# A fused attention and gated feed-forward kernel on one core: which part of w_down the second token block takes first, and where its combinations are formed

## The chip, the core and the metric

The kernel runs on one core of one Trainium2 chip. Five engines work side by side: TensorE (PE) does the matrix products, VectorE (DVE), ScalarE (ACT) and GpSimd (POOL) do the elementwise work, SyncE (SP) issues the DMAs. Matrix products land in PSUM; the other data lies in SBUF. The metric is the device time of one launch in microseconds (us), the median over several runs. The time before is 2574.85 us (three runs, 2573.92 to 2575.61).

## What is computed

All in float32, with S = 2048 tokens, D = 576, 32 heads of 18 and F = 4608:

```python
xn = layernorm(A_x)
s  = attention(xn, A_wqkv) @ A_wo              # 32 heads, softmax over all 2048 keys
g  = silu((gelu(xn @ B_w_gate) * (xn @ B_w_up)) @ B_w_down)
out = A_x + s * g
```

## The kernel before

**Tiling.** A prologue normalises x and projects q, k and v. After it, everything goes by sections. The 2048 tokens are cut into 4 blocks b of 512. The 4608 hidden columns are cut into 18 parts r of 256, each of two groups g of 128. One section is the gate and the up product of one group for one block: 27 pairs of matmuls (line 412, outputs pg and pu). There are 4 x 18 x 2 = 144 sections, in the order block, place within the block, group. Sections 11 to 138 also carry attention. Between their pairs stand eight score products (pe, line 861), whose exponential ScalarE takes (pT, line 862), and eight products for the row maxima of a later group of heads (pm, line 809), which VectorE reduces (mx, line 811). After the pairs come 32 matmuls of probabilities by values (acc, line 878). PE is programmed by hand, in the order written; in this middle stretch SP is too. The order on ACT, DVE and POOL is made there by a planner, which keeps a written order only for the instructions that are marked for it. In the epilogue all engines run in the written order.

**The ring.** pe, pm, acc and the outputs py of the down product share three PSUM buffers (`ring`, line 394). A matmul waits until an older tile has been read out of its buffer. pg and pu have two other buffers each.

**The down product.** The product with w_down is done for one part at a time, after the pairs and the acc matmuls of the section that follows the part's second group (`downs`, line 625). It goes by a scheme of seven products for a 2 x 2 split of tokens and columns (`PRODUCTS`, line 53). Seven sums of the two groups' activations (`sums_a`, `cut_a`, on POOL) meet seven combinations of the w_down quarters, held as high and low parts in the one tile T. Each of the seven py tiles is added by VectorE into one of seven accumulators M (line 527); at the first place of a later block ScalarE copies it into M instead (line 525), which starts the accumulators anew. Before that copy the accumulators of the block just finished must be combined by eight additions (`COMBINED`, line 58, done by `combine`, line 542) into four quarters of the block's result, and the quarters 6, 4, 1 and 5 must be stored to the DRAM tensor ys (line 553).

**Where T comes from.** In block 0 the first five parts (`PLAIN` = 5) are multiplied without the scheme. For the parts in `FORMED` the combinations are formed on the core. The raw w_down part is loaded (`load_rawd`), POOL makes the sums (`sums_b`, lines 475 to 477), ACT writes the high parts (`high_b`, lines 483 to 486), POOL the low parts (`low_b`, lines 491 to 494), and four DMAs store T to the DRAM tensor ts (`t_piece`, line 468). `FORMED` holds places 5 to 17 of block 0 and places 0 to 4 of block 1. Everywhere else T is loaded from ts by four DMAs.

**The turn of a block.** Place 17 of a block is multiplied after the first section of the next one. The eight additions on M are then hung into the following section and the stores behind it; the section after that ends with the copies into M. At the turns from block 1 to 2 and from 2 to 3 all eight additions go to POOL (lines 532 to 535) and all four stores are issued together. At the turn from block 0 to 1 POOL gets four of them and VectorE the other four: one at pair 14 of the same section (line 537), three at pairs 2, 8 and 13 of the section after (lines 560 and 561). The stores of quarters 1 and 5 come between the two sections, those of 6 and 4 at pair 19 of the second (line 562).

**Spare work.** From attention section `SCALED` on, every second section takes one job into two borrowed tiles: scaling an attention result, or the gate (silu) of one group of 128 rows of ys. What isn't done in this way is left to the epilogue, where `gate(k)` (line 1021) does it for row group k unless it is among the first `gated`.

**The epilogue.** It does the last sections, the last three down products and sixteen output steps. `step()` (line 1053) projects 128 rows with w_o (po, 28 matmuls, line 1036), lets VectorE multiply by the gate and add x (lines 1045 to 1050), and prepares the operand for two steps later (`split_o`: oh on ACT, ol on DVE). Lines 1161 to 1174 are the end: the last down product with eight additions on M, step 9, one gate, step 10, then the four quarters of the last block with the steps 11 to 15 between them.

Of the kernel before, what the change touches and what calls it, by code (L numbers as in the profile page):

```python
# [17 lines left out]
P = 128  # L18
NT = S // P
TB = 512  # L20
# [17 lines left out]
G = 2  # L38
NR = F // (G * P)
NF = NB * NR * G  # L40
FIRST = (0, 0, 3, 5, 3, 5, 3, 6, 4, 6, 5)
# [4 lines left out]
DC, TH = D // 2, TB // 2  # L46
ENDS = NF - len(FIRST) - NU * NA
PLAIN = len(FIRST) // G
FORMED = [(0, r) for r in range(PLAIN, NR)] + [(1, r) for r in range(PLAIN)]
NEXT = [(0, r) for r in range(1, PLAIN)] + FORMED + [(0, NR)]  # L50
OTS = (4, 9, 0, 5)
SCALED = G * (NR + PLAIN) - len(FIRST) + 1
PRODUCTS = ((2, (0, 6)), (5, (1, 3)), (3, (2, 5)), (6, (3, 4)), (0, (4, 2)), (4, (5, 1)), (1, (6, 0)))
SHARED = 8
QUARTERS = ((0, 0, 6), (0, 1, 4), (1, 0, 1), (1, 1, 5))
# [4 lines left out]
GC = 0.044715  # L60
GS = 0.7978845608028654
SCALE = DH ** -0.5


def f(ap):
# [16 lines left out]
def kernel(ctx: ExitStack, tc: tile.TileContext, x, wqkv, wo, w_gate, w_up, w_down, out):  # L82
    nc = tc.nc
# [42 lines left out]
    def load_gu(t, keep=lambda i: i):  # L126

        raw = raw_tile([P, NC, P])
        for a, w in enumerate((w_gate, w_up)):
            keep(nc.sync.dma_start(raw[HR * a:HR * a + HR], w[:, t * P:(t + 1) * P].rearrange("(k p) n -> p k n", p=HR)))  # L130
        return raw, [], []
# [382 lines left out]
    def down(b, r, then={}):  # L514
        if b == 0 and r < PLAIN:
            return down_plain()
        (ah, al), T, M = FF["A"], FF["T"], FF["M"]
        for m, (i, k) in PRODUCTS:
            py = ring("py")
            for t in range(2):  # L520
                tt = slice(t * P, (t + 1) * P)
                for n, (h, w) in enumerate(((ah, 0), (ah, 1), (al, 0))):
                    nc.tensor.matmul(py[:, t, 0:DC], h[:, i, tt], T[:, w, k], start=n == 0, stop=n == 2)  # L523
            if r == 0:
                nc.scalar.activation(M[:, m], py[:, :, 0:DC], AF.Copy)
            else:
                nc.vector.tensor_tensor(M[:, m], py[:, :, 0:DC], M[:, m], op=ALU.add)  # L527
            for eng, to, op, by in then.get(m, ()):
                eng.tensor_tensor(M[:, to], M[:, to], M[:, by], op=op)  # L529
        if r == NR - 1 and b < NB - 1:  # L530
            FF["gates"].append(b)
            for k, (p, q) in enumerate(COMBINED):
                combine_at(6 * k + 6, nc.gpsimd, q)
                if b > 0:
                    combine_at(6 * k + 6, nc.gpsimd, p)
            if b == 0:
                combine_at(14, nc.vector, COMBINED[0][0])

    def combine_at(i, eng, what):
        FF["hooks"].setdefault(i, []).append(lambda: combine(eng, *what))  # L540
# [3 lines left out]
        M = FF["M"]  # L544
        tc.keep_in_program_order(eng.tensor_tensor(M[:, to], M[:, to], M[:, by], op=op))

    def store_gates(b, some=range(7)):

        for i, c, m in QUARTERS:
            if m not in some:  # L550
                continue
            rows = slice(b * TB + TH * i, b * TB + TH * i + TH)
            nc.sync.dma_start(ys[rows, DC * c:DC * c + DC].rearrange("(t p) d -> p t d", p=P), FF["M"][:, m])

    def gates():

        for b in FF["gates"]:
            if b == 0:
                store_gates(b, (1, 5))
                for i, k in ((2, 1), (8, 2), (13, 3)):  # L560
                    combine_at(i, nc.vector, COMBINED[k][0])
                FF["hooks"].setdefault(19, []).append(lambda b=b: store_gates(b, (4, 6)))
            else:
                store_gates(b)
        FF["gates"] = []

    def load_rawd(r):
        FF["rawd"] = ffn.tile([P, G, D], F32, name="rawd")
        nc.sync.dma_start(FF["rawd"], w_down[r * G * P:(r + 1) * G * P, :].rearrange("(g p) n -> p g n", p=P))

    def section(specials=(), tag="f", slots=False, tail=0):

        n = FF["n"]
        FF["n"] += 1
        b, r = divmod(n // G, NR)
        g = n % G
        keep = tc.keep_in_program_order
        pairs, pg, pu = gate_up(tag)
        hooks, FF["hooks"] = FF["hooks"], {}

        def hook(i, what):
            hooks.setdefault(i, []).append(what)

        for i in range(n + 1, min(n + 3, NF)):
            if i not in FF["raw"]:
                FF["raw"][i] = load_gu(i % (NR * G))
        nxt = FF["raw"].pop(n + 1, None)
        one = split_ap if n + 1 < ATT.start else split
        if nxt:
            for k in range(NG - 1):  # L590
                split_gu(nxt, k, one)
        if n == 0:
            load_rawd(0)
        if g == 0 and (b, r) in FORMED:
            raw = FF["rawd"]
            hook(22 if r == 0 else 12, lambda: sums_b(raw))
        new = n + 1 < NF and (n + 1) % (NR * G) == 0
        xd = []
        if new:
            for k in range(NG - 1):  # L600
                hook(9 * k + 9, lambda k=k: xd.append(load_xd(b + 1, k)))
        for p in spread(pairs, specials, 1 if slots else None, hooks, tail):
            p()
        if nxt:
            split_gu(nxt, NG - 1, one)
        FF["w"] = nxt
        if new:
            copy_xd(xd[0], 0, keep)
        FF["act"] = activate(pg, pu, g, n < ATT.stop)
        for t in FF.pop("late", ()):  # L610
            t()
        if g > 0 or n not in ATT:
            FF.pop("last", lambda: None)()
        if new:
            xd.append(load_xd(b + 1, NG - 1, 2))
            for t in hooks.get(len(pairs), ()):
                t()
            for i in range(XG):
                FF["hooks"].setdefault(2 + 2 * i, []).append(lambda i=i: copy_xd(xd[1], 0, keep, i))
            for k in range(NG - 1):  # L620
                for i in range(XG):
                    copy_xd(xd[k], 1, keep, i)
            FF["xd"] = xd
# [5 lines left out]
    def finish():  # L629

        n = FF["n"] - 1
        b, r = divmod(n // G, NR)
        g, h = n % G, FF["act"]
        pool, vec, act = nc.gpsimd, nc.vector, nc.scalar
        keep = tc.keep_in_program_order
        FF.pop("last", lambda: None)()

        def hook(i, what):
            FF["hooks"].setdefault(i, []).append(what)

        def behind(what):
            what(keep if (n + 1) % (NR * G) == 0 else lambda i: i)

        if g == 1 and (b, r + 1) in NEXT:
            load_rawd((r + 1) % NR)
        if b == 0 and r < PLAIN:
            if g == 0:
                raw = FF["rawd"]
                hook(4, lambda: cut_plain_b(raw))
            cut_plain(g, h)  # L650
        elif (b, r) in FORMED:
            lead = n < ATT.start
            if g == 0:
                high_b(0)
                high_b(1)
                hook(2, lambda: low_b(0))
                hook(10, lambda: low_b(1))
                for k, i in enumerate((13, 20)):
                    hook(i, lambda k=k: t_piece(r, k, True))
                sums_a(g, h, vec if lead else pool)  # L660
                hook(12, lambda: cut_a(0, h, pool, pool, keep))
            else:
                for k, i in enumerate((2, 9)):
                    hook(i, lambda k=k: t_piece(r, 2 + k, True))
                behind(lambda k: (sums_a(g, h, pool, k), cut_a(1, h, pool, pool, keep)))
        else:
            if g == 0:
                late = (n + 2) % (NR * G) == 0 and n + 2 < NF
                for k, i in enumerate((None, 5, 27, 27) if late else (None, 5, 13, 21)):
                    if i is None:  # L670
                        t_piece(r, k)
                    else:
                        hook(i, lambda k=k: t_piece(r, k))
            behind(lambda k: (sums_a(g, h, pool, k), cut_a(g, h, pool, pool, k)))
        if g == G - 1:
            FF["down"].append((b, r, n + 1))
# [298 lines left out]
    with tc.tile_pool(name="epi", bufs=1, reuse_waits="tile") as epi:  # L975
# [87 lines left out]
            n += 1  # L1063

        def load_raw(n):
            FF["raw"][n] = load_gu(n % (NR * G))

        def last_section(tag):

# [87 lines left out]
        for k in range(3):  # L1157
            step()
            if k == 0:
                cut_a(1, h, act, pool)  # L1160
        last_down(2, {0: ((pool, 5, ADD, 0), (pool, 5, ADD, 2)),
                      1: ((vec, 6, SUB, 3), (vec, 6, ADD, 0), (pool, 5, SUB, 1), (vec, 6, SUB, 4), (vec, 4, ADD, 2), (pool, 1, SUB, 3))})
        step()
        gate(gated)
        step()
        M = FF["M"]
        for i, c, m in QUARTERS:
            t = ffn.tile([P, 2, DC], F32, name="tg", tag=("h0", "h1")[c], bufs=2 - c)
            act.activation(t, M[:, m], AF.Tanh, scale=0.25)
# [33 lines left out]
```

## Time and profile before

| what | value |
|---|---|
| median of three runs | 2574.85 us |
| the profiled execution's own time | 2575.34 us |
| its span, first to last instruction | 2573.6 us |
| PE busy | 2546.1 us, 99% |
| VectorE busy | 2089.8 us, 81% |
| GpSimd busy | 1640.2 us, 64% |
| ScalarE busy | 1464.9 us, 57% |

Times within the trace count from the first instruction. Matmuls are pipelined, so the end of one overlaps the start of the next, and a row's duration is that of one instruction and not its share of the engine. In a row of a timeline the bracket says how long the engine sat idle before the instruction and what released it. In a row of the windows view a stretch is followed by its length, then by busy time and count of instructions on PE, PE's weight loads, DVE, ACT and POOL, then by the granted TensorE clock as a share of full speed, the share of DMA time and GB/s. In the list of waits the numbers are us in total, times, and the longest.

### The profile page before, as it was taken

How to read it: one execution, taken by the hardware profiler on the slowest of the kernel's cores; microseconds unless marked ns; L12 is line 12 of the kernel's file. 1: busy time of each engine (PE TensorE's matmuls, PEld its weight loads, DVE VectorE, ACT ScalarE, POOL GpSimd, SP SyncE). 2: the span in 40 equal slices, each digit the busy share in tenths (PEclk: the TensorE clock that was granted, in tenths of full speed). 3: DMA queues.
4: the chain of work that ended last, by engine and by line, in shares of the span. 5: the costliest groups of instructions: out<-in, count | busy, mean ns of one | idle time of the engine just before them, and what ended most of it. 6: DMA issues, size and time to landing. Idle time of an engine off the chain costs nothing. (4 is left out here: it accounts for less than half of the span.)

```text
span 2573.6 us, 52904 instructions
## 1 busy us (share of the span) xinstructions
PE 2546.1 (99%) x20548; PEld 1838.3 (71%) x20548; DVE 2089.8 (81%) x2360; ACT 1464.9 (57%) x1772; POOL 1640.2 (64%) x1710
## 2 busy tenths in 40 slices
PE   9999999999999999999999999999999999999998
PEld 8888766676666666667766677666666776666788
DVE  5325888898887888888887898888888888888367
ACT  3224366666666656666566566555566665555621
POOL 3105588888888866666567565666667665656773
PEclk9999999999999999999999999999999999999999
DMA  8855455555575546767777666666668767665675
GB/s 263 270 184 134 103 163 160 166 166 169 159 202 171 169 136 162 170 167 167 171 185 199 168 168 169 165 169 158 162 156 210 170 169 170 170 160 152 187 210 209
DMA packets 410465, 447.47 MB, mean 174 GB/s; under 512 B 107108, under 2 KB 286820, under 8 KB 410216
## 3 DMA queue, kind: packets, MB, share of 16 engines
q1 hardware_dynamic: 410216, 444.09, 65.1%
q8 instruction: 164, 2.69, 0.5%
q14 instruction: 85, 0.70, 0.1%
HBM read 347.59 MB, written 96.38 MB: 173 GB/s over the span
## 5 line engine op out<-in xcount | busy, mean ns | idle before, releaser
L862 ACT ACTIVATE pT<-pe 128x1024 f32<-128x1024 f32 x1024 | 1047.4, 1026 | 582.6 <-PE pe L861 548.7
L811 DVE TENSOR_REDUCE mx<-pm 128x2 f32<-128x1024 f32 x1024 | 1221.4, 1224 | 179.8 <-PE pm L809 163.6
L412 PE MATMUL pu<-xd,wh 64*128 64x512 f32 x2538 | 926.5, 396 | 1.6 <-DVE t L426 1.6
L412 PE MATMUL pg<-xd,wh 64*128 64x512 f32 x2538 | 926.2, 396 | 1.9 <-ACT t L425 1.9
L412 PEld LDWEIGHTS pg<-xd,wh 64*128 64x128 f32 x2538 | 468.0, 184 | 114.3 <-issue 56.9
L412 PE MATMUL pg<-xd,wl 64*128 64x512 f32 x1269 | 496.6, 391 | 1.1 <-POOL wl L117 1.1
L412 PE MATMUL pu<-xd,wl 64*128 64x512 f32 x1269 | 496.2, 391 | 0.0
L412 PEld LDWEIGHTS pu<-xd,wh 64*128 64x128 f32 x2538 | 468.0, 184 | 29.6 <-DVE t L426 2.9
L878 PE MATMUL acc<-pT,VS 128*32 128x512 f32 x4096 | 466.0, 595 | 0.0
L110 POOL TENSOR_SCALAR wh<-raw 128x384 fp32r<-128x384 f32 x402 | 216.3, 540 | 386.1 <-PE pu L412 264.3
L112 POOL TENSOR_TENSOR wl<-raw,wh 128x384 fp32r<-128x384 f32 x402 | 414.3, 1033 | 27.8
L809 PE MATMUL pm<-KA,QT 64*128 64x512 f32 x2048 | 414.4, 394 | 6.9 <-ACT pT L862 5.0
L861 PE MATMUL pe<-QT,KA 64*128 64x512 f32 x2048 | 411.3, 393 | 4.0 <-DVE mx L811 3.7
L523 PE MATMUL py<-T,ah 128*128 128x288 f32 x1876 | 381.6, 299 | 2.2 <-DVE yy L1045 1.4
L527 DVE TENSOR_TENSOR M<-py,M 128x576 f32<-128x576 f32 x448 | 338.8, 757 | 31.9 <-PE py L523 18.2
L523 PEld LDWEIGHTS py<-T,ah 128*128 128x128 f32 x1876 | 298.8, 188 | 57.1 <-issue 55.6
L441 POOL TENSOR_TENSOR al<-h,ah 128x512 fp32r<-128x512 f32 (+1 forms) x143 | 295.6, 2067 | 64.0 <-ACT ah L438 52.4
L878 PEld LDWEIGHTS acc<-pT,VS 128*32 128x32 f32 x4096 | 120.0, 109 | 276.8 <-issue 229.8
L861 PEld LDWEIGHTS pe<-QT,KA 64*128 64x128 f32 x2048 | 193.4, 184 | 115.8 <-DVE mx L811 32.1
L523 PE MATMUL py<-T,al 128*128 128x288 f32 x938 | 276.1, 294 | 0.0
L412 PEld LDWEIGHTS pg<-xd,wl 64*128 64x128 f32 x1269 | 234.3, 185 | 31.8 <-POOL wl L117 2.0
L412 PEld LDWEIGHTS pu<-xd,wl 64*128 64x128 f32 x1269 | 234.3, 185 | 15.0
(169 smaller groups left out, 2917.5 us busy)
## 6 DMA issues: line engine op xcount, KB each, us to landing
T<-ts SPq DMA_DIRECT2D x98, 576.0 KB
KA<-qk SPq DMA_DIRECT2D x768, 72.0 KB
T<-ts SPq DMA_DIRECT2D x98, 432.0 KB
raw<-in_B_w_gate_dram SPq DMA_DIRECT2D x144, 288.0 KB
raw<-in_B_w_up_dram SPq DMA_DIRECT2D x144, 288.0 KB
ts<-T SPq DMA_DIRECT2D x36, 576.0 KB
VS<-vs SPq DMA_DIRECT2D x128, 152.0 KB
qk<-t SPq DMA_DIRECT2D x72, 256.0 KB
```

The lines of the kernel that those rows point to most:

```text
L110: first = nc.gpsimd.tensor_scalar(hi, raw, 1.0, 1.0, op0=ALU.mult, op1=ALU.mult)
L112: keep(nc.gpsimd.tensor_tensor(lo, raw, f(hi), op=ALU.subtract))
L412: nc.tensor.matmul(o, w[1 + wp][k][rr, c, :], xd[k][xp][rr, c, :], start=(i == 0), stop=(i == len(terms) - 1))
L441: keep(two.tensor_tensor(lo, raw, f(hi), op=ALU.subtract))
L523: nc.tensor.matmul(py[:, t, 0:DC], h[:, i, tt], T[:, w, k], start=n == 0, stop=n == 2)
L527: nc.vector.tensor_tensor(M[:, m], py[:, :, 0:DC], M[:, m], op=ALU.add)
L809: nc.tensor.matmul(pm[:, a], QS[u, r][rr, t * P:(t + 1) * P], KS[(u * NA + c) % KB][r][rr, :], start=True, stop=True)
L811: return nc.vector.tensor_reduce(MX[u][:, 2 * r:2 * r + 2, t, c], pm, axis=AX.X, op=ALU.max)
L861: nc.tensor.matmul(pe[:, a], KS[(u * NA + c) % KB][r][rr, t * P:(t + 1) * P], QS[u, r][rr, :], start=True, stop=True)
L862: nc.scalar.activation(PT[u, kt][:, 2 * r:2 * r + 2, :], pe, AF.Exp, scale=SCALE)
L878: nc.tensor.matmul(ACC[u][32 * a:32 * a + 32, :], VS[(u * NA + c) % VB][:, v:v + 32], pt[:, a, :], start=first, stop=last, skip_group_chec ...
```

## The change

The first place of block 1 takes part 5, whose combinations were stored in block 0; places 1 to 5 take parts 0 to 4. So place 0 of block 1 loads T, and places 1 to 5 form it. The turn from block 0 to 1 is written like the other two: eight additions on POOL, four stores together. The spare jobs start two sections later. At the end the additions on M are spread behind the steps 9 and 10, and a gate stands behind each of these two steps.

```diff
-FORMED = [(0, r) for r in range(PLAIN, NR)] + [(1, r) for r in range(PLAIN)]
-NEXT = [(0, r) for r in range(1, PLAIN)] + FORMED + [(0, NR)]
+FORMED = [(0, r) for r in range(PLAIN, NR)] + [(1, r) for r in range(1, PLAIN + 1)]
+NEXT = [(0, r) for r in range(1, PLAIN)] + FORMED
-SCALED = G * (NR + PLAIN) - len(FIRST) + 1
+SCALED = G * (NR + PLAIN + 1) - len(FIRST) + 1
+def part(b, r):
+    return r if b != 1 or r > PLAIN else r - 1 if r > 0 else PLAIN
+
+def gu_part(n):
+    return G * part(*divmod(n // G, NR)) + n % G
...
                 combine_at(6 * k + 6, nc.gpsimd, q)
-                if b > 0:
-                    combine_at(6 * k + 6, nc.gpsimd, p)
-            if b == 0:
-                combine_at(14, nc.vector, COMBINED[0][0])
+                combine_at(6 * k + 6, nc.gpsimd, p)
...
         for b in FF["gates"]:
-            if b == 0:
-                store_gates(b, (1, 5))
-                for i, k in ((2, 1), (8, 2), (13, 3)):
-                    combine_at(i, nc.vector, COMBINED[k][0])
-                FF["hooks"].setdefault(19, []).append(lambda b=b: store_gates(b, (4, 6)))
-            else:
-                store_gates(b)
+            for i, c, m in QUARTERS:
+                rows = slice(b * TB + TH * i, b * TB + TH * i + TH)
+                nc.sync.dma_start(ys[rows, DC * c:DC * c + DC].rearrange("(t p) d -> p t d", p=P), FF["M"][:, m])
...
-            hook(22 if r == 0 else 12, lambda: sums_b(raw))
+            hook(12, lambda: sums_b(raw))
...
-        g, h = n % G, FF["act"]
+        g, h, s = n % G, FF["act"], part(b, r)
...
-            load_rawd((r + 1) % NR)
+            load_rawd(part(b, r + 1))
...
-                    hook(i, lambda k=k: t_piece(r, k, True))
+                    hook(i, lambda k=k: t_piece(s, k, True))
...
-        last_down(2, {0: ((pool, 5, ADD, 0), (pool, 5, ADD, 2)),
-                      1: ((vec, 6, SUB, 3), (vec, 6, ADD, 0), (pool, 5, SUB, 1), (vec, 6, SUB, 4), (vec, 4, ADD, 2), (pool, 1, SUB, 3))})
+        last_down(2, {0: ((pool, 5, ADD, 0), (pool, 5, ADD, 2)), 1: ((vec, 6, SUB, 3), (pool, 5, SUB, 1), (vec, 6, ADD, 0))})
+        M = FF["M"]
+
+        def add(eng, to, op, by):
+            eng.tensor_tensor(M[:, to], M[:, to], M[:, by], op=op)
+
         step()
-        gate(gated)
+        add(pool, 1, SUB, 3)
+        add(vec, 6, SUB, 4)
+        gate(n)
         step()
-        M = FF["M"]
+        add(vec, 4, ADD, 2)
+        gate(n)
```

Elsewhere `load_gu(i % (NR * G))` becomes `load_gu(gu_part(i))`, and the loads from ts take `part(b, r)` in place of `r`.

More of the change, by code (lines that the diff above doesn't have):

```diff
@@ L545, in combine @@
         tc.keep_in_program_order(eng.tensor_tensor(M[:, to], M[:, to], M[:, by], op=op))
[L547 to L553, printed above, removed]
     def gates():
         for b in FF["gates"]:
-            if b == 0:
-                store_gates(b, (1, 5))
-                for i, k in ((2, 1), (8, 2), (13, 3)):
-                    combine_at(i, nc.vector, COMBINED[k][0])
-                FF["hooks"].setdefault(19, []).append(lambda b=b: store_gates(b, (4, 6)))
-            else:
-                store_gates(b)
+            for i, c, m in QUARTERS:
+                rows = slice(b * TB + TH * i, b * TB + TH * i + TH)
+                nc.sync.dma_start(ys[rows, DC * c:DC * c + DC].rearrange("(t p) d -> p t d", p=P), FF["M"][:, m])
         FF["gates"] = []
@@ L585, in section @@
             if i not in FF["raw"]:
-                FF["raw"][i] = load_gu(i % (NR * G))
+                FF["raw"][i] = load_gu(gu_part(i))
         nxt = FF["raw"].pop(n + 1, None)
@@ L663, in finish @@
                 for k, i in enumerate((2, 9)):
-                    hook(i, lambda k=k: t_piece(r, 2 + k, True))
+                    hook(i, lambda k=k: t_piece(s, 2 + k, True))
                 behind(lambda k: (sums_a(g, h, pool, k), cut_a(1, h, pool, pool, keep)))
@@ L670, in finish @@
                     if i is None:
-                        t_piece(r, k)
+                        t_piece(s, k)
                     else:
-                        hook(i, lambda k=k: t_piece(r, k))
+                        hook(i, lambda k=k: t_piece(s, k))
             behind(lambda k: (sums_a(g, h, pool, k), cut_a(g, h, pool, pool, k)))
@@ L1065, in load_raw @@
         def load_raw(n):
-            FF["raw"][n] = load_gu(n % (NR * G))
+            FF["raw"][n] = load_gu(gu_part(n))
         def last_section(tag):
```

## The prediction

> **What bounds the kernel now.** I read the busy shares first, then PE's waits around the turns of the blocks, and then measured each section from the first acc matmul of one section to that of the next.
>
> ```profile
> PE 2546.1 (99%) x20548; PEld 1838.3 (71%) x20548; DVE 2089.8 (81%) x2360; ACT 1464.9 (57%) x1772; POOL 1640.2 (64%) x1710
> ```
>
> The change adds and removes no matmul, so only stalls of PE and the clock can move the time, and 2573.6 minus 2546.1 leaves 27.5 us for all stalls, the two ends included. These are PE's waits at the turn from block 0 to 1, from 745 to 830 us:
>
> ```profile
> PE pe L861 <- DVE mx L811: 3.7, 4, 1.9
> PE pm L809 <- ACT pT L862: 2.1, 1, 2.1
> PE pe L861 <- ACT M L525: 0.3, 1, 0.3
> ```
>
> At the turn from 1 to 2 (1355 to 1430 us) and from 2 to 3 the same list is empty. A list of waits misses restarts and a lowered clock, so the windows view follows: first the four sections around the turn 0 to 1, then the four that stand at the same places of the turn 1 to 2.
>
> ```profile
> 745.27:765.18 19.91, 19.75 (x162) 14.26 (x161) 18.00 (x21) 11.97 (x15) 16.90 (x16) 1.00 0.80 243
> 765.18:783.54 18.36, 14.78 (x121) 8.45 (x119) 18.10 (x19) 9.82 (x12) 17.94 (x18) 1.00 0.71 197
> 783.54:807.87 24.33, 21.88 (x163) 17.28 (x161) 13.05 (x13) 16.03 (x22) 17.94 (x18) 0.93 0.41 121
> 807.87:821.59 13.72, 13.72 (x120) 8.72 (x119) 11.41 (x12) 10.39 (x13) 11.82 (x11) 1.00 0.72 205
> 1355.68:1375.19 19.51, 19.51 (x162) 14.30 (x161) 17.41 (x20) 9.82 (x12) 14.71 (x14) 1.00 0.86 229
> 1375.19:1388.95 13.76, 13.76 (x120) 8.65 (x118) 12.42 (x16) 9.85 (x12) 13.51 (x15) 1.00 0.65 180
> 1388.95:1408.47 19.52, 19.52 (x162) 14.24 (x160) 12.12 (x13) 14.38 (x19) 11.81 (x15) 1.00 0.79 209
> 1408.47:1422.22 13.75, 13.75 (x120) 8.64 (x119) 11.44 (x12) 10.47 (x13) 11.41 (x11) 1.00 0.36 89
> ```
>
> With nearly the same count of matmuls, the turn 0 to 1 is longer by 0.40, 4.60, 4.81 and -0.03 us, 9.78 together. That is all that making the turns alike can win.
>
> **The second section (4.60).** In it VectorE is busy 18.10 of 18.36 us, against 12.42 of 13.76 at the later turn. It is the bound there, by the three additions on M:
>
> ```profile
> 771.41 1.44 DVE L545 TENSOR_TENSOR M<-M 128x576 f32<-128x576 f32 x1
> 773.91 1.16 DVE L545 TENSOR_TENSOR M<-M 128x576 f32<-128x576 f32 x1
> 777.35 2.49 DVE L545 TENSOR_TENSOR M<-M 128x576 f32<-128x576 f32 x1
> ...
> 774.05 0.50 PE L861 MATMUL pe<-QT,KA 64*128 64x512 f32 x2 [0.84 <-DVE mx L811]
> 781.03 0.50 PE L861 MATMUL pe<-QT,KA 64*128 64x512 f32 x2 [1.85 <-DVE mx L811]
> ```
>
> Each stands ahead of a reduction, the reduction holds a ring buffer, and PE's next score product waits for it. The change takes all of these off VectorE, and the section has what its twin has: minus 4.60. The 0.40 of the first section has the same cause (the first such addition) and goes too.
>
> **Where the four additions go.** POOL does eight, as at the later turn, while place 1's forming leaves that stretch:
>
> ```profile
> 755.98 2.71 POOL L491 TENSOR_TENSOR T<-tsum,T 128x1152 fp32r<-128x1152 f32 x1
> 760.02 0.83 POOL L493 TENSOR_TENSOR T<-tsum,T 128x288 fp32r<-128x288 f32 x1
> 760.79 1.97 POOL L494 TENSOR_TENSOR T<-rawd,T 128x576 fp32r<-128x576 f32 x1
> 786.91 1.27 POOL L477 TENSOR_TENSOR tsum<-rawd 128x288 f32<-128x288 f32 x1
> ...
> 1365.99 11.18 POOL L545 TENSOR_TENSOR M<-M 128x576 f32<-128x576 f32 x8
> ```
>
> Gone are 2.71 + 0.83 + 1.97 = 5.51 us of low parts, come are four additions at 11.18 / 8 = 1.40, 5.59. The sums of that first place, just before, go too. So POOL ends the sums of place 2 (788.18 before) at the same time or earlier. PE comes there 0.40 + 4.60 = 5.0 earlier than before, and ScalarE, which began to read these sums at 793.75 (below), wants them at 788.75. The cover shrinks from 5.6 to 0.6 us if POOL ends no earlier; I cost it at nothing, as the forming that left is 4 us of cover more. The loads of T for place 1, on SP's queue, replace the stores of T, as at the later turn, where PE waits for none; the raw part for place 2 is loaded in both versions. Section lengths at places 1 to 5 of block 1 show no wait for forming, so moving it by one place costs nothing. The spare jobs run under PE, and one fewer of them fits in.
>
> **The third section (4.81).** The rows are those of ACT, then PE, then SP, then the window of lowered clock:
>
> ```profile
> 793.20 0.65 ACT L525 ACTIVATE M<-py 128x576 f32<-128x576 f32 x1 [1.15 <-PE py L523]
> 793.75 1.16 ACT L483 ACTIVATE T<-tsum 128x1152 fp32r<-128x1152 f32 x1
> ...
> 795.71 1.01 ACT L862 ACTIVATE pT<-pe 128x1024 f32<-128x1024 f32 x1
> 796.61 1.19 ACT L525 ACTIVATE M<-py 128x576 f32<-128x576 f32 x2
> ...
> 793.91 0.50 PE L861 MATMUL pe<-QT,KA 64*128 64x512 f32 x2 [0.31 <-ACT M L525]
> 796.78 0.56 PE L809 MATMUL pm<-KA,QT 64*128 64x512 f32 x2 [2.15 <-ACT pT L862]
> ...
> 782.14 0.90 SPq L553 DMA_DIRECT2D ys<-M x2
> ...
> 798.10:801.50 3.40, 3.40 (x19) 3.40 (x17) 1.85 (x3) 2.02 (x2) 3.32 (x4) 0.51 0.09 30
> ```
>
> Two of the seven copies into M come last, after the exponential. They are two whose quarter is still being stored (the two stores at 782.14), as far as the order tells; until then they hold two of the three ring buffers, so that PE waits 0.31 and then 2.15 us. Right after that wait PE runs at half clock for 3.40 us, which costs 1.70. The rest, 4.81 - 2.46 - 1.70 = 0.65, is two restarts of 0.33.
>
> After the change the stores go together and early, so the copies run in order and the ring is not blocked. But place 2 (part 0) is still formed behind the same seven copies, so ScalarE still has the high parts to write between them and the first exponential, which the later turn has not. There the copies end at 1399.06 and the fourth ring tile is wanted at 1400.50:
>
> ```profile
> 1396.82 2.24 ACT L525 ACTIVATE M<-py 128x576 f32<-128x576 f32 x3 [0.16 <-PE py L523]
> ...
> 1400.50 0.40 PE L809 MATMUL pm<-KA,QT 64*128 64x512 f32 x2
> ```
>
> Put 795.71 - 793.75 = 1.96 of high parts and 1.01 of exponential behind 1399.06: the buffer comes free at 1402.03, a wait of 1.53 and a restart of 0.33, 1.9 in all. Bounds: 0 if the planner puts the exponential first or the high parts into gaps, 4.81 if all stays as it is. I take 1.9, with no lowered clock: the 1.85 us wait at 781.03 brought none, the 2.15 did. So this section gives 2.9 of its 4.81.
>
> [...]
>
> **The end.** Here the additions on M stand ahead of VectorE's part of step 9:
>
> ```profile
> L529 DVE TENSOR_TENSOR M<-M x4: 749/1875/1885, 2541.6 to 2546.2; 128x576 f32<-128x576 f32 x4
> ...
> 2541.62 6.49 DVE L529 TENSOR_TENSOR M<-M 128x576 f32<-128x576 f32 x4
> 2548.03 0.74 DVE L1045 SCALAR_TENSOR_TENSOR yy<-yy,po 128x576 f32<-128x576 f32 x1
> 2549.48 0.68 DVE L1019 TENSOR_TENSOR ol<-KA,oh 128x512 fp32r<-128x512 f32 x1
> 2550.09 0.75 DVE L1026 SCALAR_TENSOR_TENSOR yy<-th,yy 128x576 f32<-128x576 f32 x1
> ...
> 2540.19 7.30 POOL L529 TENSOR_TENSOR M<-M 128x576 f32<-128x576 f32 x4 [5.29 <-DVE M L527]
> ...
> 2550.22 0.40 PE L1036 MATMUL po<-woh,ol 128*128 128x288 f32 x1 [1.63 <-DVE ol L1019]
> ...
> 2550.22 18.54 PE po L1036 x138
> ```
>
> PE loses 1.63 us waiting for ol; it wanted it at 2548.6. After the change two additions stand ahead of it: 0.75 + 1.87 from 2541.62 to 2544.27, yy 0.74 to 2545.0, then the addition of x and ol, each 0.7 alone and up to 1.88 beside POOL's additions, which last until 2547.5: ol at about 2548.2, no wait. Then come one addition, one gate and step 10 (2548.03 to 2550.16 is 2.13 for a step): 0.75 + 0.75 + 2.13, 2551.8. PE, at 18.54 / 5 = 3.71 a step, wants that ol at 2552.3. Next 0.75 + 0.75 + 0.75 (addition, second gate, first quarter) and 2.13: 2556.2, wanted at 2556.0, a wait of 0.2 or so. The second gate is one more VectorE operation of 0.75. I take a gain of 1.3; the bounds are a gain of 1.8 and a loss of 1.0, if every SBUF addition of these two steps is held up by POOL.
>
> **Sum.** 0.40 + 4.60 - 0.03 + 2.9 + 1.3 = 9.2 us off the profiled execution's 2575.34: 2566.2. That execution stands 0.5 above the median of the runs, so against 2574.85 it is 8.7 us, 0.34%.
>
> **The rivals.** (a) *ScalarE's burst stays whole*, with its wait and the half clock, since place 2 is formed in both versions: for it speaks that the exponential stood behind the high parts; against it, that two late copies held the buffers. Then 4.97 + 1.3 = 6.3 come off: 2569.1. [...] (b) *The burst vanishes too*, the planner fitting the high parts in: 9.78 + 1.3 come off, 2564.3. (c) *The end gives nothing back or loses, and the order elsewhere shifts against it*: VectorE's second gate makes two ol late, plus 1.0, and the burst stays: 2575.34 - 4.97 + 1.0 = 2571.4, within 0.2%. (d) *Slower: POOL becomes the bound at the turn.* If the eight additions push the sums of place 2 back, ScalarE's in-order queue holds the exponential behind the high parts, and PE stops. It decides from 0.6 us of lateness on if POOL ends no earlier than now, and costs one us for each further; to undo 9.2 and lose 5.2 more takes 15 us, a whole section of slip: 2580.5. Against it stand POOL's equal loads above and the later turn's 13.51 busy of 13.76 with no wait.
>
> **How the numbers follow.** Forecast 0.56, (a) 0.20, (b) 0.10, (c) 0.10, (d) 0.04. A difference of 0.2%, 5.15 us, is about what a measurement of this kernel tells from none; 2569.7 is that line. The forecast, (b) and somewhat over half of (a) lie below it: faster 0.76, same 0.19, slower 0.05. The range runs from 2563.5 (rival (b) with the larger gain at the end) to 2570.3, which takes in (a) with the end at nothing.
>
> **What would show it.** Right: no DVE rows on line 545; the four sections at 19.5, 13.8, about 21.4 and 13.7 us; the copies into M all ahead of the first exponential; no window of half clock; no PE wait of 1.6 on ol near the end. Wrong: the second section still above 14.5, a third section of 24, POOL's sums ending after ScalarE wants them, or new waits on ol that exceed 1.6.

## The result, and the profile after

The changed kernel takes 2562.84 us (median of five runs, 2562.28 to 2563.54) against 2574.68 for the kernel before (five runs, 2573.73 to 2575.61). The ratio is 0.9955, its 95% interval 0.9940 to 0.9969, so the change saves 11.8 us, with 8.0 to 15.4 us inside the interval. The forecast was 2566.2 with a range from 2563.5 to 2570.3. The direction was right, but the time lies 0.7 us below the range: the gain was bigger than forecast. The forecast gain of 9.2 us lies inside the interval of the gain, so it is the traces that have to tell where the rest came from.

These are the four sections around the turn from block 0 to 1 in the profile after, in the windows view, each from the first acc matmul of a section to that of the next. In this document "the first trace" is the profile before that the prediction reads:

```profile
743.91:763.42 19.51, 19.51 (x163) 14.23 (x161) 17.42 (x20) 9.83 (x12) 16.79 (x16) 1.00 0.92 267
763.42:777.16 13.74, 13.74 (x120) 8.56 (x118) 12.43 (x16) 9.85 (x12) 12.66 (x15) 1.00 0.85 224
777.16:798.25 21.09, 19.77 (x162) 14.22 (x161) 12.28 (x13) 16.13 (x22) 18.46 (x19) 1.00 0.38 120
798.25:811.96 13.71, 13.71 (x120) 8.61 (x118) 11.40 (x12) 10.42 (x13) 11.86 (x12) 1.00 0.74 197
```

They were 19.91, 18.36, 24.33 and 13.72. The first two are now as long as their twins at the later turn (19.51 and 13.76 before), VectorE's busy time in the second has come down from 18.10 to 12.43, and the granted clock is 1.00 in all four. The third is 1.57 longer than its twin of 19.52. Its rows, ACT first and then PE's one wait of size:

```profile
781.89 5.34 ACT L533 ACTIVATE M<-py 128x576 f32<-128x576 f32 x7 [2.36 <-PE py L531]
787.13 1.16 ACT L491 ACTIVATE T<-tsum 128x1152 fp32r<-128x1152 f32 x1
...
789.09 1.93 ACT L855 ACTIVATE pT<-pe 128x1024 f32<-128x1024 f32 x2
...
790.15 0.51 PE L802 MATMUL pm<-KA,QT 64*128 64x512 f32 x2 [1.32 <-ACT pT L855]
```

All seven copies into M now run in one go. Behind them stand the high parts of place 2, and behind these the exponential for which PE waits 1.32 us; 2.15 and a lowered clock stood there before. On POOL the eight additions take 11.16 us and the sums of place 2 end at 782.46, 4.7 us before ScalarE begins to read them:

```profile
753.02 11.16 POOL L550 TENSOR_TENSOR M<-M 128x576 f32<-128x576 f32 x8
...
781.66 0.80 POOL L485 TENSOR_TENSOR tsum<-rawd 128x288 f32<-128x288 f32 x1
```

At the end, VectorE has two additions ahead of step 9, and then waits for PE itself (the bracket at 2534.70). The last row is from the chain that ended last: the seven output steps run without a break, at 25.97 / 7 = 3.71 us a step.

```profile
2531.66 2.65 DVE L537 TENSOR_TENSOR M<-M 128x576 f32<-128x576 f32 x2
2534.70 0.76 DVE L1038 SCALAR_TENSOR_TENSOR yy<-yy,po 128x576 f32<-128x576 f32 x1 [0.38 <-PE po L1029]
2536.16 1.92 DVE L1012 TENSOR_TENSOR ol<-KA,oh 128x512 fp32r<-128x512 f32 x1
...
2530.95 25.97 PE po L1029 x196
```

### The profile page after: what moved, and what is told of

Same layout as the page of the kernel before. It is cut to its first block, busy times and chain, and to the rows that moved or that the text cites. A ratio compares the mean times of both kernels' runs of the same rounds, so it can differ in the third digit from the quotient of the medians.

```text
span 2561.5 us, 52902 instructions
## 1 busy us (share of the span) xinstructions
PE 2541.3 (99%) x20548; PEld 1846.6 (72%) x20548; DVE 2076.9 (81%) x2357; ACT 1465.8 (57%) x1772; POOL 1643.5 (64%) x1712
## 4 chain that ended last, share of the span: by engine, by line
PE 94%; DMA 2%; POOL 1%; DVE 1%; ACT 1%; issue 1%; SPq 0%; POOLq 0%; DVEq 0%; ACTq 0%
PE pg L420 28%; PE acc L871 18%; PE py L531 14%; PE pm L802 9%; PE pe L854 9%; PE po L197 7%; PE pu L420 6%; PE po L1029 1%; PE py L518 1%; DMA xx<-in_A_x_dram 0%; DMA raw<-in_B_w_up_dram 0%; DMA raw<-in_B_w_gate_dram 0%; PE pt L258 0%; DMA T<-ts 0%; ACT pT L855 0%
## 5 line engine op out<-in xcount | busy, mean ns | idle before, releaser
L535 DVE TENSOR_TENSOR M<-py,M 128x576 f32<-128x576 f32 x448 | 339.0, 758 | 32.2 <-PE py L531 19.5
L802 PEld LDWEIGHTS pm<-KA,QT 64*128 64x128 f32 x2048 | 202.4, 184 | 50.4 <-ACT pT L855 10.4
```

What stands on the lines that cost most here:

```text
L802: nc.tensor.matmul(pm[:, a], QS[u, r][rr, t * P:(t + 1) * P], KS[(u * NA + c) % KB][r][rr, :], start=True, stop=True)
```

## The experiments

The question after the result was where the gain beyond the forecast came from. PE runs the same 20,548 matmuls in the same order in every one of these kernels, so two traces can be laid over each other matmul by matmul. Against the first trace of the kernel before, the trace after is 8.3 us shorter at the turn and 1.9 at the end, 10.2 together; the rest, 1.9 of the 12.1 us between the two spans, lay in small pieces all over. Theory 1: the change works at these two places alone, and what is left is what differs between executions. Theory 2: the change also makes the undisturbed sections, those away from the turn and the end, quicker.

### The two kernels again, and each half of the change alone

The kernels `b_same` and `a_same` are the two kernels unchanged. `turn_only` is the changed kernel with the old order at the end; since its spare jobs do one gate fewer, both gates stand behind step 9:

```diff
-        last_down(2, {0: ((pool, 5, ADD, 0), (pool, 5, ADD, 2)), 1: ((vec, 6, SUB, 3), (pool, 5, SUB, 1), (vec, 6, ADD, 0))})
+        last_down(2, {0: ((pool, 5, ADD, 0), (pool, 5, ADD, 2)),
+                      1: ((vec, 6, SUB, 3), (vec, 6, ADD, 0), (pool, 5, SUB, 1), (vec, 6, SUB, 4), (vec, 4, ADD, 2), (pool, 1, SUB, 3))})
...
         step()
-        add(pool, 1, SUB, 3)
-        add(vec, 6, SUB, 4)
-        gate(n)
+        gate(10)
+        gate(11)
         step()
-        add(vec, 4, ADD, 2)
-        gate(n)
```

`end_only` is the kernel before with the new end, that is, with the last part of the change's diff alone.

> The kernel before, unchanged, once more. Theory 1 (the change works through its stalls alone, and the 2 us by which it beat the forecast beyond them are the pace of an execution): this trace's undisturbed sections, for example the 464 us from acc of section 43 to that of section 75, differ from those of the first trace of this kernel by some 0.1% either way, and its ratio to before is 1.000. Theory 2 (the change itself makes the undisturbed sections quicker by 0.1%): this trace has the pace of the first one within 0.02%. The half clock behind the turn from block 0 to 1 may be there or not, 1.7 us.

> The changed kernel, unchanged, once more. Both theories: 2562.8 within 1 us, ratio 0.9954. Theory 1: the half clock of 3.4 us in the epilogue (after the wait of 2.0 us of a py product on VectorE's yy) can be gone, and then the end of the trace is some 1.7 us shorter; the pace of the undisturbed sections can differ from the other trace of this kernel by up to 0.1%. Theory 2: the pace is again 0.1% quicker than that of the kernel before run beside it.

> Block 1's first place takes part 5 and the turn from block 0 to 1 is as in the change, but the end has the old order of additions, with both gates behind step 9. Theory 1: the turn gives 8 us with half clock and 7 without, the end loses the second gate (0.75 on VectorE ahead of step 10's multiply): 2566.5 to 2567.5, ratio 0.997, and a wait on ol of 1.6 to 2.4 us near the end. Rival (the end brings nothing): 2562.8 as the whole change.

> The turn and the forming as before, only the end has the new order; one gate there does nothing, since its row group is done earlier. Theory 1: the wait of 1.63 us on ol goes, nothing takes its place: 1.8 us less than before, 2572.9, ratio 0.9993. Rival (the end brings nothing, or gives it back in waits on ol of the next two steps): 2574.7, ratio 1.000.

Measured, beside the kernel before at 2576.28 us: `b_same` 2577.56, ratio 1.0004 (0.9995 to 1.0013); `a_same` 2564.32, ratio 0.9957 (0.9944 to 0.9969); `turn_only` 2566.69, ratio 0.9965 (0.9953 to 0.9977); `end_only` 2575.32, ratio 1.0000 (0.9991 to 1.0009).

The gain repeats: `a_same` stands 12.0 us below the kernel before that ran beside it, though its own time of 2564.32 us lies inside the forecast range, since that kernel took 2576.28 here. The turn alone has most of the gain. The end's 1.9 us is less than `end_only` can resolve by its time, but the traces show it: in `turn_only` PE still waits for ol near the end, as in this list of its waits from 2525 us on, and in `end_only` the same list has the second line alone.

```profile
PE po L1029 <- DVE ol L1012: 1.6, 1, 1.6
PE py L531 <- DVE M L535: 0.5, 1, 0.5
```

Matched matmul by matmul, the stretch of twelve matmuls that holds this wait is 3.43 to 3.48 us long in every trace with the old end (3.47 in the first trace) and 1.57 or 1.58 in every trace with the new one. The second gate in `turn_only` added nothing there (3.47 again), against the 0.75 expected.

Theory 2 is neither shown nor excluded. From attention section 28 to section 60 (807.87 to 1340.14 us in the first trace), where nothing was changed but the places of the parts and the start of the spare jobs, the traces of the kernel before and of `end_only` have 532.27, 532.97 and 532.16 us, those with the new turn 531.72, 532.10 and 532.11. The further executions below have 531.87 and 532.21 with the old turn and 532.05 with the new one, so the ranges overlap. The means differ by 0.3 us, where Theory 2 had 0.1%, 0.5 us, and the traces of the kernel before alone by 1.1.

### More executions

The surprise was in the turn itself: the trace of `end_only`, whose turn is that of the kernel before, lost 0.8 us more there than the first trace. `b2`, `b3` and `a2` are the two kernels unchanged once more, for their traces.

> The kernel before, once more, for its trace. Theory 1 (the waits at its turn sit at the edge of what halves the clock, so that the executions differ by how often it does): one to three windows of half clock of 3.41 us each between 760 and 800 us, 24 to 30 us over the two sections' undisturbed 33.3 less what the waits explain; the undisturbed sections at the pace of the other traces of this call within 0.05%. Rival (the half clock behind the third section is there in every execution and nothing else): one window, at 797 us.

> The same as b2, another execution. Theory 1: the count of half clock windows at the turn need not be that of b2. Rival: one window, at 797 us, again.

> The changed kernel, once more, for its trace. Theory 1: no half clock at the turn (its one wait of 1.3 us lies below the 1.85 us that brought none), the turn 8.26 us shorter than in the first trace of the kernel before; a window of half clock may be there near 2500 us, behind the wait on VectorE's yy. Rival: a half clock at the turn in this execution.

Measured, one time each: 2579.3, 2576.54 and 2565.44 us. The three sections of the turn in `b2` and then in `b3`, in the windows view (the last three columns are clock, DMA share and GB/s):

```profile
745.81:765.85 20.04, 19.80 (x163) 14.23 (x161) 18.09 (x21) 12.01 (x15) 17.23 (x16) 1.00 0.82 242
765.85:785.92 20.07, 16.09 (x120) 9.62 (x118) 17.67 (x19) 10.05 (x12) 19.65 (x19) 0.91 0.71 202
785.92:810.20 24.28, 21.83 (x162) 16.97 (x160) 12.23 (x13) 15.90 (x21) 16.36 (x17) 0.93 0.35 104
```

```profile
745.64:769.09 23.45, 21.16 (x162) 15.30 (x161) 20.20 (x21) 12.15 (x15) 21.67 (x19) 0.93 0.66 189
769.09:784.78 15.69, 14.54 (x121) 8.53 (x119) 14.65 (x19) 9.78 (x12) 13.32 (x15) 1.00 0.80 219
784.78:809.08 24.30, 21.86 (x162) 17.02 (x160) 12.94 (x13) 16.02 (x22) 17.95 (x18) 0.93 0.41 128
```

The clock is below 1.00 in two sections of each, where the first trace had it in one. The third section and its half clock are the same in all five traces of the old turn (24.16 to 24.33 us, behind a wait of 2.13 to 2.15); it is the first two that differ. In `b2` it falls after a wait of 1.87 us on a reduction; the first trace had a wait of 1.85 us at the same matmul, and its clock stayed. In `b3` it falls a section earlier, behind an addition on M that took 2.93 us there and 0.79 in the first trace. These are PE's wait in `b2`, and VectorE's addition and PE's wait in `b3`:

```profile
781.84 0.51 PE L861 MATMUL pe<-QT,KA 64*128 64x512 f32 x2 [1.87 <-DVE mx L811]
```

```profile
761.03 2.93 DVE L545 TENSOR_TENSOR M<-M 128x576 f32<-128x576 f32 x1
...
765.16 0.79 PE L861 MATMUL pe<-QT,KA 64*128 64x512 f32 x2 [2.29 <-DVE mx L811]
```

Why one wait lowers the clock and another does not, these traces do not show. The length of the wait does not tell the two apart: the clock falls behind the 1.87 us in `b2` (0.51 from 782.40 to 785.81) and the 2.29 us in `b3` (0.51 from 764.80 to 768.20), and it stays at 1.00 behind the 1.85 us in the first trace and behind a wait of 2.63 us at the same matmul in `b_same`. This is that wait, and the section that holds it:

```profile
781.69 0.50 PE L861 MATMUL pe<-QT,KA 64*128 64x512 f32 x2 [2.63 <-DVE mx L811]
...
765.02:784.21 19.19, 14.51 (x121) 8.53 (x119) 17.69 (x19) 9.84 (x12) 18.69 (x19) 1.00 0.65 186
```

All traces of the two turns, in us from acc to acc:

| trace | first | second | third | together | stretches of half clock |
|---|---|---|---|---|---|
| before, first trace | 19.91 | 18.36 | 24.33 | 62.60 | 1 |
| `b_same` | 19.91 | 19.18 | 24.16 | 63.25 | 1 |
| `b2` | 20.04 | 20.07 | 24.28 | 64.39 | 2 |
| `b3` | 23.45 | 15.69 | 24.30 | 63.44 | 2 |
| `end_only` | 23.41 | 15.70 | 24.30 | 63.41 | 2 |
| after, first trace | 19.51 | 13.74 | 21.09 | 54.34 | 0 |
| `a_same` | 19.50 | 13.77 | 21.05 | 54.32 | 0 |
| `a2` | 19.48 | 13.77 | 21.10 | 54.35 | 0 |
| `turn_only` | 19.53 | 13.74 | 21.05 | 54.32 | 0 |

The new turn takes the same time within 0.03 us in every execution; the old one varies by 1.8, and the trace from which I predicted is the cheapest of the five. Their mean is 63.42, so the turn gives 63.42 - 54.33 = 9.1 us on average, not 8.3.

### Is it the additions, the forming, or the stores?

The kernel `adds_only` is the kernel before with the additions and stores of the change, and the forming left at places 0 to 4:

```diff
-                if b > 0:
-                    combine_at(6 * k + 6, nc.gpsimd, p)
-            if b == 0:
-                combine_at(14, nc.vector, COMBINED[0][0])
+                combine_at(6 * k + 6, nc.gpsimd, p)
...
-            if b == 0:
-                store_gates(b, (1, 5))
-                for i, k in ((2, 1), (8, 2), (13, 3)):
-                    combine_at(i, nc.vector, COMBINED[k][0])
-                FF["hooks"].setdefault(19, []).append(lambda b=b: store_gates(b, (4, 6)))
-            else:
-                store_gates(b)
+            store_gates(b)
```

`late_store` is the changed kernel with quarters 6 and 4 of block 0 stored as before, at pair 19 of the second section. `move_only` is `late_store` with the four additions put back on VectorE as well, so that of the change only the moved forming and the end are left:

```diff
+            store_gates(b, (1, 5) if b == 0 else range(7))
+            if b == 0:
+                for i, k in ((2, 1), (8, 2), (13, 3)):
+                    combine_at(i, nc.vector, COMBINED[k][0])
+                FF["hooks"].setdefault(19, []).append(lambda b=b: store_gates(b, (4, 6)))
```

The two lines with `combine_at`, and the one at pair 14 as before, are in `move_only` alone.

> The kernel before, with all eight additions of the turn from block 0 to 1 on POOL and its four stores together; the forming stays at places 0 to 4 and the end is as before. Theory 1 (the additions on VectorE and the late stores are the whole cause; the forming need not move): the second section 13.8 us, the third 21.1, the turn 8.3 us shorter, 2566.5 or ratio 0.9968. Rival (POOL cannot take the four additions of 1.40 us beside place 0's low parts of 5.5 us: it ends the sums of place 1 at 789 to 794 instead of 783, ScalarE's high parts wait for them and PE behind these): the second section 13.8 to 16, the third 23 to 27, and the turn gives 0 to 4 us.

> The changed kernel, with the turn's additions and stores as before: four additions on VectorE, quarters 6 and 4 stored at pair 19 of the second section. The forming is moved and the end is new. Theory 1: moving the forming alone gives nothing, the second section 17.5 to 18.5 us, the third 23 to 24.5, only the end gives 1.9: 2572.8 or ratio 0.9993. Rival (the load on POOL was the cause, and VectorE's additions are short once POOL leaves them alone): the second section 16 us, the third 21, 2567 to 2569.

> The changed kernel with one edit: quarters 6 and 4 of block 0 are stored at pair 19 of the second section instead of ahead of it. Theory 1 (the late stores put two of the seven copies into M behind the exponential, and these hold two ring buffers): second section 13.8 us, third 22.5 to 24.5 instead of 21.1, with two copies in the timeline after the first exponential, and the half clock behind it in some executions: 1.5 to 3.5 us more than the changed kernel, ratio 0.9967 to 0.9973. Rival (the copies run in order all the same, and the wait came from the slow reductions before): third section 21.1, ratio 0.9957 as the changed kernel.

Measured, beside 2575.42 for the kernel before: `adds_only` 2573.95, ratio 0.9991 (0.9980 to 1.0001); `move_only` 2570.48, ratio 0.9978 (0.9969 to 0.9986); `late_store` 2568.45, ratio 0.9971 (0.9960 to 0.9982). Of each, the second and third section of the turn:

```profile
765.26:788.09 22.83, 16.80 (x120) 10.80 (x119) 12.67 (x16) 9.82 (x12) 22.41 (x23) 0.78 0.63 180
788.09:809.26 21.17, 19.85 (x163) 14.31 (x161) 12.57 (x13) 16.13 (x22) 17.45 (x18) 1.00 0.39 120
```

```profile
765.65:781.35 15.70, 14.53 (x121) 8.54 (x119) 14.68 (x19) 9.88 (x12) 12.27 (x13) 1.00 0.68 174
781.35:806.82 25.47, 23.02 (x162) 17.96 (x160) 13.04 (x13) 16.02 (x22) 17.93 (x18) 0.87 0.38 112
```

```profile
764.61:778.37 13.76, 13.76 (x120) 8.60 (x118) 12.51 (x16) 9.87 (x12) 12.88 (x15) 1.00 0.77 189
778.37:802.39 24.02, 21.57 (x163) 16.22 (x161) 12.34 (x13) 16.05 (x22) 18.57 (x19) 0.93 0.42 130
```

*The forming has to move.* In `adds_only` (the first fence) POOL is busy 22.41 of 22.83 us of the second section, the clock's mean is 0.78, and the section is 4.5 us longer than before although VectorE's busy time is down to 12.67. Neither theory had the way it goes. POOL also writes the row maxima (m), as a rounded copy and its low part, in two operations of 0.2 us, and VectorE transposes them. They now stand behind the additions, VectorE waits for them with its reductions queued behind the transpose, and PE waits for a reduction. The rows are POOL's, VectorE's and PE's:

```profile
769.46 5.58 POOL L542 TENSOR_TENSOR M<-M 128x576 f32<-128x576 f32 x4
...
778.59 0.22 POOL L817 TENSOR_TENSOR m<-nm,m 128x16 fp32r<-128x16 f32 x1
...
778.84 0.21 DVE L822 STREAM_TRANSPOSE mt<-m 128x32 f32<-128x32 f32 x1 [6.16 <-POOL m L817]
...
780.21 0.79 PE L852 MATMUL pe<-QT,KA 64*128 64x512 f32 x2 [6.03 <-DVE mx L802]
```

In the changed kernel those additions are done at 764.2 and the second of the two small operations at 768.9. Rival (d) of the prediction, POOL as the bound at the turn, is thus a true danger, one engine further along than I had it, and the moved forming is what averts it. The third section of `adds_only`, 21.17, has the early stores and is as short as in the changed kernel.

*The moved forming alone helps VectorE, as far as one trace tells.* In `move_only` (the second fence) VectorE's three additions in the second section take 0.80, 0.74 and 1.13 us against 1.44, 1.16 and 2.49 in the first trace, and the section is 15.70 us. The expectation of 17.5 to 18.5 was wrong. It is not that POOL has less to do beside these additions: `b3` and `end_only`, where the forming is not moved, have the same section of 15.7 us with the same durations. What the three share is that POOL has emptied its queue. It starts its first product on h 3.2 us into the section, after a wait for VectorE, where in the first trace it came to it without a wait and 5.8 us into the section, and so other operations of POOL lie beside the additions. In `b3` and `end_only` a late first section gave POOL the time, in `move_only` the low parts that went elsewhere. The third section, with late stores, is 25.47 in this execution (23 to 24.5 expected), with half clock for 6.83 us (0.87 on average over the section), so that by its trace this turn is only 1.1 us shorter than in the first trace before; by the ratio of its runs the kernel is 5.7 us quicker than the one before (3.6 to 8.0), the end included.

*The late stores are the cause in the third section.* In `late_store` (the third fence) the second section stays at 13.76, and the third goes back from 21.09 to 24.02, where 22.5 to 24.5 was expected. As in the kernel before, two copies into M come behind the exponential, and PE waits (ACT and then PE):

```profile
790.50 1.01 ACT L861 ACTIVATE pT<-pe 128x1024 f32<-128x1024 f32 x1
791.40 1.19 ACT L533 ACTIVATE M<-py 128x576 f32<-128x576 f32 x2
...
791.56 0.86 PE L808 MATMUL pm<-KA,QT 64*128 64x512 f32 x2 [2.14 <-ACT pT L861]
```

### What is left: forming from place 2 on

In `form_two` places 0 and 1 of block 1 take parts 5 and 6, and the first five parts are formed at places 2 to 6, away from the copies into M. In `form_two_b` the spare jobs start no later for that, and no third gate goes to the end.

```diff
-FORMED = [(0, r) for r in range(PLAIN, NR)] + [(1, r) for r in range(1, PLAIN + 1)]
+FORMED = [(0, r) for r in range(PLAIN, NR)] + [(1, r) for r in range(2, PLAIN + 2)]
...
-    return r if b != 1 or r > PLAIN else r - 1 if r > 0 else PLAIN
+    return r if b != 1 or r > PLAIN + 1 else r - 2 if r > 1 else PLAIN + r
```

`form_two` has besides `SCALED` higher by G, and `gate(9)` behind step 7.

> The changed kernel, with places 0 and 1 of block 1 given to parts 5 and 6 and the first five parts formed at places 2 to 6; the spare jobs start two sections later again, and one more gate goes to the end, behind step 7. Theory 1 (what is left of the third section's wait is ScalarE's high parts between the copies and the first exponential): third section 19.5 us as at the later turns, no PE wait at the turn, 1.6 us less than the changed kernel, ratio 0.9951, if the third gate hides under PE. Rival (the wait is of the copies themselves, or the gate at the end costs what the turn gives): 21.1 us or a new wait near the end, ratio 0.9957 or above.

> As form_two (places 0 and 1 of block 1 take parts 5 and 6, the first five are formed at places 2 to 6), but the spare jobs start where they do in the changed kernel, so that no third gate goes to the end. Theory 1 (the 3.7 us at 1337 us in form_two was one late DMA with a half clock behind it, and its 0.9 us at the end the third gate): third section 19.5 us, nothing new at the later turns, the end as in the changed kernel: 1.6 us less than that, ratio 0.995. Rival (moving by two places delays the loads at the next turn): again 1 to 4 us near 1337 us, ratio 0.996.

Measured: `form_two` 2566.44 us, ratio 0.9963 (0.9950 to 0.9975) beside 2575.42 before; `form_two_b` 2564.52 us, ratio 0.9958 (0.9945 to 0.9972) beside 2575.13 before. Ratios of 0.9951 and 0.995 were expected. The third section is 19.5 us in both; this is its row in `form_two_b`:

```profile
778.60:798.07 19.47, 19.47 (x162) 14.35 (x160) 12.09 (x13) 14.38 (x19) 9.91 (x13) 1.00 0.66 183
```

So the remaining 1.6 us of the turn do come from ScalarE's high parts between the copies and the exponential. Whether the version is faster as a whole isn't shown. The ratio of `form_two_b` lies on that of the changed kernel (0.9955 and 0.9957), and its span, 2563.2 us, lies among those of the three traces of the changed kernel (2561.5, 2562.3 and 2563.5). So the 1.6 us are lost again outside the turn. In `form_two` 3.7 us went near 1337 us behind a late DMA (PE waits 1.1 us for it and 1.8 for ScalarE's xd), which `form_two_b` didn't repeat. That one waits 1.9 us on yy in the epilogue, but the first trace of the changed kernel has the same wait with 2.0 us; the rest lies in small pieces that differ between executions.

## Why the prediction was right in kind and short in size

| step | forecast, us off | measured against the first trace |
|---|---|---|
| first section | 0.40 | 19.91 - 19.51 = 0.40 |
| second section | 4.60 | 18.36 - 13.74 = 4.62 |
| third section | 2.9 | 24.33 - 21.09 = 3.24 |
| the end | 1.3 | 3.47 - 1.57 = 1.90 |
| sum | 9.2 | 10.2 |

**The step that failed** is the first one: that the turn's excess over its twin, 9.78 us of one execution, "is all that making the turns alike can win". It was read as a fixed price, and the bounds hang on it: by the prediction's own terms no more than 9.78 + 1.8 = 11.6 us could come off (2563.8 us; the range begins a little lower, at 2563.5), and 11.8 did by the medians, although 1.57 us of the third section stayed. The five traces show that the old turn costs 0 to 1.8 us more than in that execution, 0.82 on average, as the reductions keep PE waiting for different times (3.5 to 4.7 us over the turn) and the clock falls once or twice and at one place or another. With 9.1 for the turn and 1.9 for the end the sum is 11.0, within the interval of 8.0 to 15.4 around the 11.8 measured.

The reasoning on the clock failed in the same place. "The 1.85 us wait at 781.03 brought none, the 2.15 did" took the outcome of one execution for a bound on length. `b2` has 1.87 at that matmul and half clock behind it; `b_same` has a wait of 2.63 at that matmul and no half clock behind it. A stretch of half clock is 3.41 us long in the first trace (0.50 from 798.05 to 801.46) and in `b2`, and 6.83 us in `move_only`; what it takes to set one off, beyond the waits that stand ahead of them, is not shown. The half clock of the third section, which I had put at 1.70 us, is there in all five traces (0.93 on average over that section). What the reasoning left out is that a wait with no half clock behind it in one trace can have one in another, and that is what counted.

**Two terms were mis-sized** on the first trace itself. The third section gave 3.24 for 2.9, since the wait that stayed is 1.32 with 0.25 of restart, for 1.53 and 0.33. The end gave 1.90 for 1.3. That term took the 1.63 us of the wait without its restart of 0.27, and counted some new waits on ol. There are none: the stretches of the two following steps are the same in both versions within 0.02 us, and VectorE waits for PE at 2534.70. The second gate costs nothing.

**The starting point** was high as well. The forecast time was counted down from the profiled execution's 2575.34 us, which is 0.66 above the median of 2574.68; that alone is as much as the time lies below the range.

**The rest held.** The second section was VectorE's, by the additions on M. The two late copies came from the late stores, which was a reading of the order only and is shown by `late_store`. The high parts of place 2 were left, as `form_two` shows. POOL had the room, with 4.7 us between its sums and ScalarE (forecast 0.6 or more); `adds_only` shows that it has it only because the forming moved. Of the rivals, (a) and (b) were each a bound of the third section, and it came out between them.

**Open** is the difference of 0.8 us between the sum and the medians, and with it Theory 2. Outside the turn and the last seven output steps, the five traces of the old turn take 2483.0 to 2485.1 us and the four of the new one 2481.0 to 2483.1, on average 1.9 less. Of this 1.2 lies in the epilogue ahead of those steps. There PE waits for yy at one down product: 1.42 us in the first trace, with no half clock behind it, and 1.44 us in `b2` and 2.01 in the trace after, with one behind each (0.50 from 2516.30 to 2519.71, and from 2501.40 to 2504.80). Whether the change has a part in this or only the executions differ is not shown.

## What to carry to other kernels

Price a stall at a place where the clock can fall from several executions, and take the mean: one trace shows one outcome, and a repair that takes all waits away from such a place wins the average of all of them, and a steadier time with it. Here the one wait that stays in the new turn, 1.32 us, had no lowered clock behind it in any of its four traces. When work is moved to another engine, look not only at that engine's busy share but at the smallest thing in its queue that someone else needs soon: here two operations of 0.2 us behind four additions cost PE a wait of 6 us. And when buffers are copied out in an order that a planner chooses, a store that reads the target late can reorder the copies and hold the ring: PE waited 2.14 us for that in `late_store`.

## What the runs showed that I had not expected

The same addition on VectorE, 128 x 576 in SBUF, took 0.74 to 3.26 us in the traces of the kernel before, by what POOL did beside it, as far as the first trace tells: at one and the same place 0.79 in the first trace and 2.93 in `b3`. In the first trace the three that took longer, 1.44, 1.16 and 2.49 us, end at 772.85, 775.07 and 779.84, each 0.61 to 0.62 us after the end of a two-input operation of POOL that was running when they began (772.24, 774.45 and 779.22), which leaves less than the 0.74 of the shortest one:

```profile
770.95 1.29 POOL L450 TENSOR_TENSOR h<-h,h 128x512 f32<-128x512 f32 x1
773.73 0.72 POOL L452 TENSOR_TENSOR h<-h 128x256 f32<-128x256 f32 x1
776.27 2.95 POOL L441 TENSOR_TENSOR al<-h,ah 128x1280 fp32r<-128x1280 f32 x1
```

Small shifts between executions so become waits of PE of different lengths: behind the addition of 2.93 us in `b3` stands the wait of 2.29.

A loss can also shorten what follows. In `b3` and `end_only` the first section lost 3.5 us to a wait of 2.3 us and the half clock behind it, and the second was 15.7 us instead of 18.36, with shorter additions (0.74 to 1.13 us). The turn as a whole was then only 0.8 us dearer than in the first trace.
